# One seven-bank accumulator tile becomes four tiles, with the order list and the slot list made anew

## The chip, the cores and the metric

The kernel runs on one core of one Trainium2 chip. The metric is device microseconds of one execution, from the first to the last instruction of the program with what lies around them. The time before is 926.73 us, the median of 3 runs (922.49 to 929.71).

## The reference, cut to what matters

Attention inside hash buckets, then a mixture-of-experts step for the 128 best tokens of each batch:

```
q_bits, k_bits = (q @ proj > 0), (k @ proj > 0)          # proj: 64 x 6, so 64 buckets
mask   = bucket(q)[:, None] == bucket(k)[None, :]
scores = where(mask, q @ k.T / 8, -1e9)                  # 32 heads, 768 x 768
attn   = exp(scores - max) / (sum + 1e-9);  o = attn @ v  # 768 x 64 per head
x      = heads side by side                               # 4 batches, 768 x 512
top    = 128 best of x @ w_gate, per batch
out    = x;  out[top] += sigmoid(score) * (relu(x[top] @ w1) @ w2)   # w1 512 x 1024, w2 1024 x 512
```

## The kernel before, in words

All matmul results live in PSUM, eight banks of 512 fp32 columns. One bank is the tile `av` (output of attention). The other seven are one tile named `seven` (L198). `bank()` (L200) hands out one bank of it, `bank2()` (L203) two banks, which need not be neighbours; which ones is read digit by digit from the string BANKS.

The work is a list of short words in the string ORDER, 1955 of them, run from left to right. Each word calls a small function that issues a few instructions; each engine executes its own instructions in exactly that order, and an engine that waits holds up everything behind it. A framework adds the waits between engines from the tiles that the instructions read and write. No loop stands around the heads: words of neighbouring heads are mixed by hand or by a planner. For head h the words are:

- `xh`, `xl` (L413, L418): the fp32 input X is split in a high and a low fp16 part, on ScalarE (ACT) and VectorE (DVE). `h`, `sg`, `ss` hash four heads at once (TensorE L333, ACT L342, DVE L358). `ps`, `pa`, `pb` are DMAs on SyncE's queue (L425) that put signs, high parts and low parts into the operand buffers A (four of them) and B (three). `kv` (L518) forms on DVE the difference of the two halves of the keys.
- `mx`, `re`, `ma`, `rd`, three times each: the row maxima. `mx` (TensorE L526, two matmuls of 385 columns) takes two banks; `re` (ACT L533) is a relu in place; `ma` (TensorE L542) adds two more matmuls to the same banks, which gives the larger of the two halves; `rd` (DVE L552) takes the maximum of each row. `mt` (TensorE L560, one bank), `mc2` (ACT L565) and the DMA `mr` turn the maxima into a row of A.
- `s`, `e`, six times each: scores minus maximum. An even `s` (TensorE L586 and L589, four matmuls of 512 columns) takes two banks and is read by `e` (ACT L606, exp); an odd one (four of 256 columns) takes one bank (ACT L602). The result is P in SBUF.
- `r` (DVE L619) or `g` (GpSimd, POOL, L622): the low part R of P. `a`, six times (TensorE L644, 18 matmuls of 65 columns, with one of 396 columns, L631, ahead of the first): attention output into `av`. `rc`, `nw` (DVE) divide.
- `sv`, `sh`, `sl` for every second head: sums of v (TensorE L482, one bank).
- `w`, `c0` to `c3`, `e0` to `e3`: pieces of generators that load weights, choose the 128 tokens of a batch and run the expert on them (L872, L894: matmuls of 128 and 512 columns; one bank for each of their results). Those of the last batch come after all heads.

Of the kernel before, what the change touches and what calls it, by code (L numbers as in the profile page):

```python
# [52 lines left out]
re.1.2 ps.2.0 ma.1.1 ia.3 rd.1.1 s.0.0 ma.1.2 s.0.2 ps.2.1 xh.4 pb.2.1 rd.1.2 kv.2 e.0.0 r.0.0 s.0.3 e.0.2 X.15
ps.3.0 ps.3.1 e.0.3 s.0.4 mt.1 mc2.1 s.0.5 xl.4 mx.2.1 mx.2.2 e.0.4 re.2.1 pb.1.0 a.0.0 xl.6 mx.2.0 re.2.2 e.0.5
pb.3.3 ma.2.1 re.2.0 a.0.1 ma.2.2 mr.1 rd.2.1 s.1.1 X.7 s.1.4 e.1.1 xh.7 g.0.1 pb.3.0 rd.2.2 ma.2.0 s.1.3 s.1.0
V.1 pb.3.2 rd.2.0 e.1.4 kv.3 mt.2 e.1.0 r.0.2 mc2.2 a.0.2 s.1.2 xl.7 a.0.3 mx.3.1 xl.5 e.1.2 pa.4.0 s.1.5 pb.2.0
X.8 re.3.1 a.0.4 e.1.5 mx.3.2 mr.2 ma.3.1 r.1.0 e.1.3 h.1.0.4 rd.3.1 pa.4.1 s.2.5 re.3.2 ma.3.2 a.0.5 mx.3.0 w
rd.3.2 pb.4.3 sg.1.0.4 vh.1 s.2.4 pb.3.1 ss.1.0.4 rc.0 re.3.0 g.1.1 e.2.5 s.2.1 ps.4.1 e.2.4 pb.4.1 ps.5.1 ma.3.0
s.2.0 nw.0 rd.3.0 s.2.2 kv.4 mt.3 ps.4.0 s.2.3 pb.4.2 pa.5.1 e.2.0 pa.5.0 mx.4.0 vl.1 e.2.1 e.2.2 re.4.0 pa.6.1
X.11 mc2.3 pb.5.0 a.1.0 r.2.0 a.1.1 pa.6.0 pb.5.3 mx.4.1 e.2.3 re.4.1 mr.3 lg ps.6.0 r.1.2 a.1.2 sv.1 g.2.1 mx.4.2  # L60
sh.1 w pb.4.0 re.4.2 a.1.3 sl.1 ma.4.1 ma.4.0 a.1.4 V.2 rd.4.1 s.3.3 a.1.5 ps.5.0 ma.4.2 s.3.4 w rd.4.0 s.3.0
xh.11 e.3.3 X.10 rd.4.2 xh.8 s.3.1 rc.1 e.3.4 s.3.2 e.3.1 nw.1 e.3.0 mt.4 a.2.0 mc2.4 s.3.5 a.2.1 a.2.2 kv.5 e.3.2
# [1035 lines left out]
```

## Time and profile before

| | |
|---|---|
| median of 3 runs | 926.73 us |
| profiled execution, its own time | 927.88 us |
| its span, first to last instruction | 926.0 us |
| instructions | 13583 |
| TensorE matmul (PE) busy | 601.0 us |
| DVE busy | 357.2 us |
| ACT busy | 302.9 us |
| POOL busy | 130.4 us |
| mean granted TensorE clock | 0.679 of 2.4 GHz |

Busy time is the union of an engine's instructions; matmuls are pipelined and their ends are modelled, so a run of matmuls reads a little longer than what it adds to the path. The granted clock has two levels, 1.2 and 2.4 GHz, so a mean of 0.68 says that TensorE had the full clock for about a third of the time.

### The profile page before, as it was taken

To read this page: it belongs to the slowest core of one execution; us is meant where nothing else is said; L and a number is where in the kernel's file an instruction comes from. 1 tells how busy PE (TensorE), PEld (TensorE's weight loads), DVE (VectorE), ACT (ScalarE), POOL (GpSimd) and SP (SyncE) were. 2 spreads that over 40 slices of the span, in tenths; PEclk is the share of its full clock that TensorE was granted. 3 is DMA by queue.
4 is the path that set the end of the run, shared out by engine and by line. 5 is a ranking of instruction groups with operands and counts; after the bars stand their busy time and mean duration, and the time that the engine had idled before them with its cause. 6 is when DMAs were issued, how large, how long until landed. Compare 5 with 4: busy or idle time off the path is not lost.

```text
span 926.0 us, 13583 instructions
## 1 busy us (share of the span) xinstructions
PE 601.0 (65%) x5727; PEld 371.6 (40%) x5734; DVE 357.2 (39%) x585; ACT 302.9 (33%) x433; POOL 130.4 (14%) x91
## 2 busy tenths in 40 slices
...
DMA packets 32940, 53.32 MB, mean 58 GB/s; under 512 B 5226, under 2 KB 24176, under 8 KB 32880
## 3 DMA queue, kind: packets, MB, share of 16 engines
q1 hardware_dynamic: 21696, 32.92, 13.1%
...
q0 software_dynamic: 640, 2.10, 0.7%
q8 instruction: 45, 0.74, 0.3%
...
## 4 chain that ended last, share of the span: by engine, by line
PE 55%; ACT 24%; DVE 12%; issue 6%; DMA 2%; SPq 1%; ACTq 0%; POOLq 0%; DVEq 0%
PE seven L586 13%; PE seven L589 11%; ACT P L606 9%; PE av L644 9%; DVE m L552 9%; ACT seven L533 7%; PE seven L526 6%; PE seven L542 6%; ACT P L602 5%; PE seven L872 2%; PE seven L894 2%; PE seven L333 2%; DMA X<-in_qk_dram 1%; PE seven L482 1%; ACT sg L342 1%
## 5 line engine op out<-in xcount | busy, mean ns | idle before, releaser
L586 PE MATMUL seven<-A 97*128 97x256 f16 (+1 forms) x384 | 172.6, 455 | 130.6 <-DVE m L552 36.8
L552 DVE TENSOR_REDUCE m<-seven 128x2 fp32r<-128x770 f32 x96 | 91.3, 959 | 321.7 <-PE seven L542 84.5
L644 PEld LDWEIGHTS <-P 128*128 128x128 bf16 x2304 | 165.4, 117 | 35.9 <-issue 28.7
L589 PE MATMUL seven<-B 128*128 128x256 f16 (+1 forms) x384 | 176.4, 466 | 0.0
L644 PE MATMUL av<-V,P 128*128 128x65 f16 (+1 forms) x2304 | 169.5, 221 | 0.0
L622 POOL TENSOR_TENSOR R<-P 128x1536 f16<-128x1536 f32 x32 | 89.8, 2807 | 525.5 <-DVE R L619 114.7
L644 PE MATMUL av<-V,R 128*128 128x65 f16 x1152 | 161.4, 219 | 0.0
L606 ACT ACTIVATE P<-seven 128x1024 f32<-128x1024 f32 x96 | 97.4, 1022 | 184.5 <-PE seven L589 84.4
L644 PEld LDWEIGHTS <-R 128*128 128x128 f16 x1152 | 131.3, 117 | 0.0
L619 DVE TENSOR_TENSOR R<-P 128x1536 f16<-128x1536 f32 x64 | 111.9, 1751 | 49.7 <-ACT P L606 25.0
L589 PEld LDWEIGHTS <-B 128*128 128x128 f16 x384 | 46.9, 122 | 184.7 <-issue 174.7
L533 ACT ACTIVATE seven<-seven 128x770 f32<-128x770 f32 x96 | 76.5, 797 | 129.3 <-PE seven L589 40.7
L602 ACT ACTIVATE P<-seven 128x512 f32<-128x512 f32 x96 | 56.3, 596 | 168.9 <-PE seven L589 74.9
L542 PE MATMUL seven<-A 96*128 96x385 f16 x192 | 61.6, 416 | 52.7 <-ACT seven L533 23.4
L526 PE MATMUL seven<-kd,A 96*128 96x385 f16 x192 | 64.6, 439 | 36.4 <-ACT seven L533 9.3
L586 PEld LDWEIGHTS <-A 97*128 97x128 f16 x384 | 49.8, 130 | 55.4 <-issue 37.7
L542 PEld LDWEIGHTS <-A 96*128 96x128 f16 x192 | 20.3, 113 | 72.7 <-issue 62.2
L526 PEld LDWEIGHTS <-A 96*128 96x128 f16 x192 | 20.0, 117 | 52.6 <-issue 47.3
L872 PE MATMUL seven<-xth,w1h 128*128 128x128 f16 x128 | 24.3, 254 | 15.3 <-ACT P L606 4.6
L418 DVE SCALAR_TENSOR_TENSOR XL<-X,XH 128x768 f16<-128x768 f32 x32 | 31.3, 995 | 3.4 <-ACT XH L413 3.4
L413 ACT ACTIVATE XH<-X 128x768 f16<-128x768 f32 x32 | 26.5, 835 | 3.7 <-DMA X<-in_qk_dram 3.6
L872 PEld LDWEIGHTS <-w1h 128*128 128x128 f16 x256 | 23.7, 116 | 4.5 <-DVE xtl L848 2.1
...
## 6 DMA issues: line engine op xcount, KB each, us to landing
...
```

The source lines that it names most:

```text
L526: nc.tensor.matmul(pt[:, i, : HS + 1], a[0:96, 0, q0 : q0 + P], kd, start=True, stop=False, skip_group_check=True,)
L533: nc.scalar.activation(o, o, AF.Relu)
L542: nc.tensor.matmul(pt[:, i, : HS + 1], a[0:96, 0, q0 : q0 + P], a[0:96, 1, HS : S + 1], start=False, stop=True, skip_group_check=True,)
L552: nc.vector.tensor_reduce(st["m", h][:, 2 * t : 2 * t + 2], st["mx", h, t][:, :, : HS + 1], axis=AX.X, op=ALU.max)
L586: nc.tensor.matmul(o, a[:, 1, k0 : k0 + P], a[:, 0, q0 : q0 + n], start=True, stop=False,)
L589: nc.tensor.matmul(o, bt[:, 1, k0 : k0 + P], bt[:, 0, q0 : q0 + n], start=False, stop=True,)
L602: nc.scalar.activation(pp[:, :, 512:S], pt.rearrange("p (a b) -> p a b", a=2), AF.Exp, scale=ES)
L606: nc.scalar.activation(pp[:, :, 0:512], pt, AF.Exp, scale=ES)
L619: mine(nc.vector.tensor_tensor(**rest(h, g)))
L622: turn(nc.gpsimd.tensor_tensor(**rest(h, g)))
L644: nc.tensor.matmul(o[:, t, 0:n], l, vv[:, c, hh, v0 : v0 + n], start=False, stop=last and l is lo, skip_group_check=True,)
L872: nc.tensor.matmul(hp[:, j * P : (j + 1) * P], l[:, k, f : f + P], r[:, k * P : (k + 1) * P], start=first, stop=t["u", e] == 48, skip_grou ...
```

## The change: what it does, and the diff

Three things change. The tile `seven` is replaced by four tiles in the same seven banks: `two0`, `two1`, `two2` of two banks each and `one` of one bank. `bank()` now takes the first bank of any of the four, `bank2()` both banks of one of the first three. The string BANKS has one digit for each taking of a tile (377) where it had one for each bank (580). ORDER holds the same 1955 words in another order, so every instruction of before is there, none is new, and the order on each engine and each DMA queue is another.

```diff
 ORDER = """
...
-V.14 rd.28.2 kv.29 e.27.3 pb.28.1 a.25.5 c2 s.27.2 rc.25 nw.25 c2 s.27.5 mt.28 e.27.2 e.27.5 s.27.4 s.27.0 mc2.28
...
+c2 e.27.0 pa.30.0 ps.30.1 s.27.3 c2 s.27.2 kv.29 ps.29.0 pb.29.1 e.27.3 c2 mt.28 a.25.4 s.27.4 c2 mc2.28 r.26.0
...
 BANKS = """
-0123401423 5601240163 5012453624 3560312450 6513206213 0634512340 6534125634 1201345602 1301235641 2035146213
...
+2131203102 1320310321 2032310302 1320300230 1231302301 2102310132 1302130221 2310213203 2130121303 2012312030
...
     banks = iter("".join(BANKS.split()))
-    seven = pp7.tile([P, 7, 512], F32, name="seven")
+    slots = [pp7.tile([P, 2, 512], F32, name=f"two{i}") for i in range(3)]
+    slots.append(pp7.tile([P, 1, 512], F32, name="one"))

     def bank(name=None):
-        return seven[:, int(next(banks))]
+        return slots[int(next(banks))][:, 0]

     def bank2(name=None):
-        i, j = sorted((int(next(banks)), int(next(banks))))
-        return seven[:, i : j + 1 : j - i]
+        return slots[int(next(banks))][:, 0:2]
```

A stretch of the new order, for one head's worth of work, with the tile that each word takes in brackets (0 to 2 are `two0` to `two2`, 3 is `one`; DMA words left out): mx.10.1[0] re.10.1 rd.9.0 rc.6 g.7.1 s.8.5[3] s.8.0[1] ma.10.1 rd.9.2 e.8.5 e.8.0 mx.10.0[2] mt.9[3] mc2.9 nw.6 a.7.0 s.8.3[3] a.7.1 e.8.3 rd.10.1 mx.10.2[0] a.7.2 xl.12 s.8.2[1] a.7.3 re.10.0 r.8.2 a.7.4 a.7.5 re.10.2 e.8.2 r.8.0 ma.10.0 ma.10.2 kv.11 rc.7.

## Rows read from the trace of the kernel before

**Rows 1.** The page's head: span; an engine's busy time, share, instructions
```profile
span 926.0 us, 13583 instructions
...
PE 601.0 (65%) x5727; PEld 371.6 (40%) x5734; DVE 357.2 (39%) x585; ACT 302.9 (33%) x433; POOL 130.4 (14%) x91
```

**Rows 2.** The chain that ended last: shares by engine, then by line
```profile
PE 55%; ACT 24%; DVE 12%; issue 6%; DMA 2%; SPq 1%; ACTq 0%; POOLq 0%; DVEq 0%
PE seven L586 13%; PE seven L589 11%; ACT P L606 9%; PE av L644 9%; DVE m L552 9%; ACT seven L533 7%; PE seven L526 6%; PE seven L542 6%; ACT P L602 5%; PE seven L872 2%; PE seven L894 2%; PE seven L333 2%; DMA X<-in_qk_dram 1%; PE seven L482 1%; ACT sg L342 1%
```

**Rows 3.** Groups of instructions by line: busy us, mean ns | idle before, releaser
```profile
L552 DVE TENSOR_REDUCE m<-seven 128x2 fp32r<-128x770 f32 x96 | 91.3, 959 | 321.7 <-PE seven L542 84.5
...
L533 ACT ACTIVATE seven<-seven 128x770 f32<-128x770 f32 x96 | 76.5, 797 | 129.3 <-PE seven L589 40.7
```

**Rows 4.** Who waited for whom: us in total, times, longest us
```profile
DVE m L552 <- PE seven L542: 84.5, 25, 10.2
DVE m L552 <- PE seven L589: 62.4, 18, 8.8
DVE m L552 <- ACT P L602: 39.4, 12, 9.2
ACT P L602 <- DVE m L552: 31.2, 10, 4.8
ACT P L606 <- PE seven L526: 24.8, 13, 3.8
PE seven L542 <- ACT seven L533: 23.4, 20, 3.4
```

**Rows 5.** Timeline from 433 to 442: start, us, engine, line [idle before <-releaser]
```profile
433.26 1.02 ACT L606 ACTIVATE P<-seven 128x1024 f32<-128x1024 f32 x1 [1.79 <-PE seven L872]
434.33 0.49 PE L526 MATMUL seven<-kd,A 96*128 96x385 f16 x2 [0.56 <-ACT P L606]
434.85 1.02 ACT L606 ACTIVATE P<-seven 128x1024 f32<-128x1024 f32 x1 [0.57 <-PE seven L526]
435.93 0.22 PE L872 MATMUL seven<-xth,w1h 128*128 128x128 f16 x1 [1.11 <-ACT P L606]
...
437.83 1.63 ACT L533 ACTIVATE seven<-seven 128x770 f32<-128x770 f32 x2
...
441.15 0.51 SPq L425 DMA_DIRECT2D A<-XH  x1
```

**Rows 6.** Stretches: PE, PEld, DVE, ACT, POOL busy (instructions); PEclk, DMA share, GB/s
```profile
0.00:44.00 44.00, 18.12 (x98) 9.03 (x99) 17.58 (x31) 17.48 (x22) 11.20 (x35) 0.74 0.44 125
44.00:886.00 842.00, 562.88 (x5442) 345.72 (x5448) 327.41 (x518) 282.72 (x405) 117.25 (x54) 0.67 0.19 54
872.00:886.00 14.00, 12.92 (x239) 9.94 (x239) 6.64 (x24) 2.54 (x3) 3.75 (x2) 0.91 0.01 2
886.00:926.00 40.00, 20.01 (x187) 16.87 (x187) 12.17 (x37) 2.74 (x6) 1.96 (x2) 0.74 0.17 60
```

**Rows 7.** Pieces of the chain in order of time: start, us, what
```profile
29.52 2.12 PE seven L333 x12
...
409.77 1.34 PE seven L872 x24
...
413.57 0.34 PE seven L526 x2
...
861.12 0.54 PE av L644 x18
...
862.10 0.22 PE seven L586
...
872.17 0.33 PE av L631
...
901.33 20.25 issue
```

**Rows 8.** The tile seven, one line's instructions: ns minimum/median/maximum
```profile
L606 ACT ACTIVATE P<-seven x96: 996/1023/1035, 49.7 to 877.0; 128x1024 f32<-128x1024 f32 x96
```

More of the change, by code (lines that the diff above doesn't have):

```diff
@@ L53 @@
[L53 to L62, printed above, removed]
@@ new lines @@
+xh.7 e.1.2 ps.3.1 kv.3 e.1.3 X.8 s.1.0 mt.2 xl.7 mc2.2 a.0.2 s.1.5 vh.1 a.0.3 mx.3.1 h.1.0.4 e.1.0 re.3.1 r.0.2
+mr.2 mx.3.2 X.11 ma.3.1 e.1.5 a.0.4 sg.1.0.4 s.2.3 X.10 w vl.1 rd.3.1 pa.4.0 ss.1.0.4 mx.3.0 r.1.0 re.3.2 e.2.3
+s.1.4 a.0.5 e.1.4 ps.5.1 pb.3.1 rc.0 ps.4.0 pb.4.3 s.2.1 ma.3.2 re.3.0 ps.4.1 xh.9 s.2.4 e.2.4 w ma.3.0 nw.0
+rd.3.2 a.1.0 e.2.1 a.1.1 s.2.5 rd.3.0 g.1.1 kv.4 s.2.0 pb.3.0 r.1.2 e.2.5 mt.3 mx.4.2 V.2 s.2.2 mc2.3 a.1.2 a.1.3
+r.2.2 w mr.3 pa.6.1 e.2.0 mx.4.1 re.4.2 e.2.2 re.4.1 ma.4.2 ps.5.0 a.1.4 s.3.5 pa.5.0 pa.5.1 ma.4.1 r.2.0 w e.3.5
@@ new lines @@
+rd.4.2 w pb.5.0 mx.4.0 kv.5 X.22 a.1.5 sv.1 g.2.1 pb.4.2 s.3.2 rd.4.1 re.4.0 vh.2 sh.1 e.3.2 rc.1 pb.4.1 s.3.0
+sl.1 nw.1 ma.4.0 s.3.3 s.3.1 e.3.0 a.2.0 e.3.1 rd.4.0 mt.4 ps.6.1 w s.3.4 pa.7.0 e.3.3 a.2.1 pb.5.3 mc2.4 mx.5.1
+r.3.0 xl.9 e.3.4 mx.5.2 a.2.2 re.5.1 pb.4.0 mx.5.0 mr.4 ma.5.1 re.5.2 pa.7.1 pb.5.2 a.2.3 ps.7.0 re.5.0 pa.6.0
+vl.2 kv.6 ma.5.2 a.2.4 rd.5.1 ma.5.0 pb.6.2 rd.5.2 xh.11 sv.2 s.4.3 s.4.4 lg w a.2.5 g.3.1 e.4.3 sh.2 rd.5.0 X.15
+mt.5 sl.2 ps.6.0 rc.2 s.4.5 e.4.4 mc2.5 e.4.5 s.4.0 xh.8 s.4.2 w xl.11 s.4.1 pb.5.1 mx.6.2 e.4.0 mr.5 pb.6.3 e.4.2
@@ new lines @@
+nw.2 a.3.0 re.6.2 r.3.2 mx.6.0 r.4.2 ps.7.1 mx.6.1 xl.8 a.3.1 e.4.1 re.6.0 re.6.1 ma.6.2 w a.3.2 xh.10 rd.6.2
+s.5.5 pb.6.0 ma.6.0 a.3.3 V.3 kv.7 g.4.1 a.3.4 rd.6.0 mx.7.0 ma.6.1 re.7.0 rd.6.1 s.5.1 e.5.1 a.3.5 ma.7.0 w rc.3
+pb.7.3 nw.3 e.5.5 mt.6 s.5.4 mc2.6 s.5.0 e.5.4 s.5.3 rd.7.0 pb.6.1 mr.6 vh.3 pb.7.2 r.4.0 e.5.0 s.6.2 s.5.2 w
+xl.10 pb.8.3 e.6.2 po.0.0 a.4.0 h.2.0.4 e.5.3 a.4.1 sg.2.0.4 mx.7.1 a.4.2 w s.6.5 a.4.3 pa.8.0 r.5.0 pa.9.1 X.14
+pa.9.0 r.5.2 ss.2.0.4 ps.9.0 a.4.4 s.6.4 re.7.1 e.5.2 e.6.5 vl.3 ps.8.1 pb.7.1 mx.7.2 ma.7.1 pa.8.1 rd.7.1 a.4.5 w
@@ new lines @@
+e.6.4 ps.8.0 pb.8.2 rc.4 s.6.3 g.5.1 s.6.1 nw.4 re.7.2 e.6.3 ma.7.2 pb.7.0 s.6.0 e.6.1 pb.8.0 sv.3 rd.7.2 xh.15
+kv.8 X.16 sh.3 a.5.0 e.6.0 a.5.1 mx.8.2 mt.7 pb.9.2 mx.8.1 a.5.2 sl.3 V.4 mc2.7 mx.8.0 pb.9.0 r.6.2 re.8.2 mr.7
+a.5.3 ma.8.2 ps.9.1 w pa.10.1 re.8.0 re.8.1 r.6.0 ps.10.1 xh.14 pa.10.0 a.5.4 ma.8.0 rd.8.2 pb.9.3 s.7.3 w ps.10.0
+kv.9 ma.8.1 e.7.3 s.7.0 a.5.5 rd.8.1 w rd.8.0 s.7.5 s.7.1 e.7.0 vh.4 g.6.1 mx.9.1 e.7.5 rc.5 re.9.1 nw.5 s.7.2
+e.7.1 a.6.0 ma.9.1 a.6.1 e.7.2 s.7.4 mt.8 a.6.2 mx.9.0 pb.8.1 w a.6.3 vl.4 pb.10.2 xl.14 r.7.0 mc2.8 a.6.4 mr.8 w
@@ new lines @@
+e.7.4 pa.11.0 ps.11.1 mx.9.2 rd.9.1 w re.9.0 s.8.4 re.9.2 ma.9.0 s.8.1 X.12 r.7.2 e.8.4 pb.9.1 xl.15 w ps.11.0
+a.6.5 ma.9.2 pb.10.3 e.8.1 kv.10 xh.12 mx.10.1 X.17 re.10.1 rd.9.0 rc.6 pa.11.1 g.7.1 pb.10.1 s.8.5 s.8.0 ma.10.1
+rd.9.2 e.8.5 e.8.0 mx.10.0 mt.9 mc2.9 pb.10.0 nw.6 X.13 a.7.0 mr.9 s.8.3 a.7.1 e.8.3 rd.10.1 mx.10.2 a.7.2 V.5
+xl.12 s.8.2 a.7.3 re.10.0 r.8.2 a.7.4 a.7.5 re.10.2 e.8.2 r.8.0 pb.11.3 ma.10.0 ma.10.2 kv.11 rc.7 xh.13 sv.4 w
+s.9.4 sh.4 pb.11.2 vh.5 rd.10.0 s.9.0 pb.11.1 sl.4 pa.12.1 s.9.3 e.9.4 pb.11.0 mx.11.1 e.9.0 e.9.3 nw.7 a.8.0
@@ new lines @@
+re.11.1 g.8.1 rd.10.2 mt.10 c0 s.9.2 a.8.1 mc2.10 s.9.5 w e.9.5 xl.13 c0 ma.11.1 h.3.0.4 e.9.2 rd.11.1 s.9.1 vl.5
+mx.11.0 pa.12.0 c0 mr.10 e.9.1 a.8.2 pa.13.1 c0 re.11.0 mx.11.2 c0 a.8.3 ma.11.0 a.8.4 s.10.5 c0 re.11.2 r.9.0
+ma.11.2 w a.8.5 c0 sg.3.0.4 ss.3.0.4 rd.11.0 rc.8 s.10.0 xh.16 w ps.12.1 s.10.4 g.9.1 e.10.5 s.10.3 nw.8 rd.11.2
+a.9.0 e.10.0 a.9.1 e.10.4 sv.5 s.10.1 mt.11 mc2.11 c0 c0 a.9.2 ps.12.0 s.10.2 mr.11 kv.12 pb.13.3 ps.13.1 sh.5
+r.9.2 a.9.3 e.10.3 pa.14.1 e.10.1 sl.5 pb.12.0 e.10.2 mx.12.2 r.10.0 s.11.2 ps.13.0 c0 re.12.2 e.11.2 a.9.4 s.11.5
@@ new lines @@
+c0 w e.11.5 pb.12.2 ma.12.2 pb.12.3 mx.12.0 rd.12.2 c0 re.12.0 mx.12.1 c0 a.9.5 ma.12.0 pb.13.2 ps.14.1 g.10.1
+re.12.1 pa.13.0 s.11.4 ma.12.1 rd.12.0 e.11.4 V.6 rc.9 nw.9 c0 pb.13.1 c0 rd.12.1 pb.12.1 pa.14.0 s.11.0 s.11.1
+a.10.0 a.10.1 kv.13 e.11.1 mt.12 mx.13.1 c0 e.11.0 a.10.2 s.11.3 mc2.12 mx.13.0 pb.13.0 re.13.1 r.10.2 mr.12
+e.11.3 ma.13.1 pb.14.1 ps.14.0 rd.13.1 a.10.3 mx.13.2 ps.15.1 s.12.3 re.13.0 pa.15.0 re.13.2 ma.13.0 s.12.2 e.12.3
+r.11.0 e.12.2 a.10.4 ma.13.2 xh.17 a.10.5 rd.13.0 c0 s.12.5 rd.13.2 w g.11.1 c0 s.12.1 s.12.0 rc.10 nw.10 r.11.2
@@ new lines @@
+e.12.1 vh.6 e.12.0 a.11.0 e.12.5 s.12.4 a.11.1 X.18 kv.14 mx.14.1 e.12.4 a.11.2 mt.13 r.12.0 pb.15.0 e0 mx.14.2
+vl.6 re.14.1 mc2.13 ma.14.1 a.11.3 pa.16.0 a.11.4 pb.15.2 sv.6 e0 pa.16.1 mx.14.0 w rd.14.1 mr.13 re.14.2 pb.14.2
+ma.14.2 ps.15.0 g.12.1 sh.6 w rd.14.2 s.13.1 re.14.0 a.11.5 pa.15.1 X.19 ma.14.0 w s.13.0 rc.11 sl.6 w pb.14.0
+kv.15 rd.14.0 e.13.1 nw.11 xh.18 s.13.4 s.13.3 e.13.0 s.13.5 e.13.3 mx.15.0 xh.19 pb.15.3 a.12.0 r.12.2 e.13.5
+mt.14 xl.19 xl.17 a.12.1 e.13.4 a.12.2 mc2.14 mx.15.2 pb.14.3 X.27 xl.16 re.15.0 a.12.3 s.13.2 re.15.2 a.12.4 V.7
@@ new lines @@
+pa.17.1 w a.13.5 rd.16.0 e.15.2 vh.8 mx.16.2 ps.17.1 kv.17 re.16.2 rc.13 e0 pb.16.0 nw.13 s.15.1 e0 pa.18.1 s.15.0
+e.15.1 ma.16.2 w g.15.1 pb.16.1 s.15.4 r.14.0 e.15.0 pa.18.0 ps.19.1 rd.16.2 a.14.0 ps.18.1 a.14.1 e0 w mt.16 vl.8
+e0 mx.17.2 a.14.2 mc2.16 a.14.3 e.15.4 e0 pb.17.0 mx.17.0 xh.22 re.17.2 r.15.2 mr.16 re.17.0 ma.17.2 V.9 a.14.4
+s.16.3 pa.19.0 w pb.18.2 pb.18.3 X.21 a.14.5 rd.17.2 e.16.3 e0 mx.17.1 re.17.1 ma.17.0 r.15.0 s.16.0 ma.17.1
+pb.17.3 pb.17.1 kv.18 e0 rc.14 rd.17.0 s.16.1 ps.19.0 nw.14 e.16.0 mx.18.2 rd.17.1 e0 pa.19.1 e.16.1 a.15.0 e0
@@ new lines @@
+xh.21 X.24 s.16.2 mt.17 mx.18.1 re.18.2 ma.18.2 mc2.17 re.18.1 xh.20 a.15.1 r.16.0 pb.18.0 s.16.5 rd.18.2 a.15.2
+mx.18.0 ma.18.1 e.16.2 a.15.3 xl.21 re.18.0 mr.17 a.15.4 kv.19 xl.22 ma.18.0 e.16.5 mx.19.1 sv.8 rd.18.1 po.1.0
+rd.18.0 sh.8 a.15.5 s.16.4 sl.8 vh.9 rc.15 e.16.4 nw.15 s.17.3 re.19.1 s.17.0 a.16.0 e.17.3 X.25 a.16.1 s.17.2
+g.16.1 pb.19.3 vl.9 ma.19.1 r.16.2 c1 rd.19.1 a.16.2 e.17.0 pb.19.2 c1 mx.19.2 X.28 mt.18 a.16.3 e.17.2 g.17.1
+re.19.2 c1 xl.20 s.17.4 s.17.1 mc2.18 pb.19.1 pb.19.0 pb.18.1 e.17.4 a.16.4 ma.19.2 mr.18 mx.19.0 rd.19.2 e.17.1
@@ new lines @@
+a.18.0 rd.20.2 e.19.4 pb.21.0 a.18.1 mx.21.1 mt.20 r.18.2 e.19.1 e.19.3 c1 mc2.20 re.21.1 pb.20.3 ps.22.1 mx.21.2
+c1 a.18.2 mx.21.0 c1 re.21.2 mr.20 ps.22.0 ma.21.1 c1 re.21.0 pb.21.3 ma.21.2 vh.10 kv.22 a.18.3 c1 ma.21.0
+rd.21.1 c1 c1 pb.21.2 a.18.4 xh.24 rd.21.2 rd.21.0 s.19.5 g.19.1 s.19.0 e.19.5 s.20.3 pa.23.1 a.18.5 s.20.5 e.19.0
+mt.21 mc2.21 mr.21 rc.18 s.20.2 e.20.5 pa.23.0 s.20.0 s.20.4 e.20.3 s.20.1 e.20.2 nw.18 r.19.0 pa.24.0 e.20.4
+a.19.0 mx.22.2 e.20.0 mx.22.0 pb.22.2 re.22.0 ps.23.1 a.19.1 vl.10 re.22.2 ps.23.0 s.21.0 ma.22.0 e.20.1 a.19.2
@@ new lines @@
+r.19.2 e.21.0 a.19.3 r.20.2 ma.22.2 c1 xh.27 sv.10 rd.22.0 mx.22.1 pb.23.3 pb.22.0 sh.10 re.22.1 xh.26 c1 r.20.0
+a.19.4 s.21.3 g.20.1 sl.10 e.21.3 rd.22.2 a.19.5 ma.22.1 s.21.2 rc.19 nw.19 s.21.4 e.21.2 s.21.5 pb.23.2 pb.22.3
+rd.22.1 kv.23 e.21.4 xl.26 a.20.0 s.21.1 pa.25.1 xl.27 mt.22 mc2.22 mx.23.1 xl.24 xl.25 pa.24.1 a.20.1 a.20.2
+e.21.5 mx.23.0 re.23.1 ma.23.1 e.21.1 e1 X.30 a.20.3 pb.23.1 pb.22.1 mr.22 rd.23.1 pa.25.0 re.23.0 e1 h.6.0.4 X.31
+ma.23.0 a.20.4 mx.23.2 rd.23.0 sg.6.0.4 e1 s.22.1 s.22.0 a.20.5 re.23.2 pb.24.1 r.21.0 e1 e1 ma.23.2 ss.6.0.4
@@ new lines @@
+e.22.1 g.21.1 V.11 s.22.3 rc.20 e1 e.22.0 s.22.5 vh.11 rd.23.2 e1 ps.24.1 pb.24.0 mt.23 mc2.23 pb.23.0 nw.20
+e.22.3 vl.11 e.22.5 a.21.0 kv.24 xh.30 e1 s.22.4 w ps.24.0 sv.11 a.21.1 X.29 mr.23 r.21.2 e.22.4 s.23.0 sh.11 e1
+mx.24.0 a.21.2 e.23.0 a.21.3 mx.24.1 sl.11 ps.25.1 re.24.0 re.24.1 a.21.4 ma.24.0 r.22.2 a.21.5 s.23.5 mx.24.2
+re.24.2 ma.24.1 rd.24.0 rd.24.1 s.22.2 ma.24.2 e.23.5 kv.25 e1 e1 xh.29 e1 V.12 e.22.2 rd.24.2 mt.24 ps.26.1
+pb.24.3 s.23.3 r.22.0 ps.25.0 pb.24.2 rc.21 mc2.24 pa.26.1 nw.21 e.23.3 e1 s.23.4 s.23.2 vh.12 e.23.4 e.23.2
@@ new lines @@
+pb.25.1 a.22.0 g.22.1 ps.26.0 a.22.1 mr.24 mx.25.0 r.23.2 g.23.1 re.25.0 mx.25.1 pb.25.2 a.22.2 vl.12 re.25.1
+a.22.3 a.22.4 s.23.1 ma.25.1 ma.25.0 e1 s.24.5 pb.25.0 e.23.1 rd.25.1 e1 pa.26.0 r.23.0 s.24.3 e.24.5 mx.25.2
+e.24.3 pb.25.3 xl.29 V.13 e1 s.24.4 e1 re.25.2 ma.25.2 a.22.5 kv.26 pb.26.3 e1 rd.25.0 e.24.4 rd.25.2 xh.31 s.24.2
+pa.27.0 r.24.2 e.24.2 s.24.0 e1 rc.22 e.24.0 pa.27.1 sv.12 sh.12 nw.22 s.24.1 a.23.0 xl.30 mx.26.1 e1 e.24.1 e1
+sl.12 mt.25 re.26.1 mx.26.2 e1 r.24.0 xh.28 ps.27.1 pb.27.3 mc2.25 re.26.2 ma.26.1 mx.26.0 ma.26.2 a.23.1 re.26.0
@@ new lines @@
+a.23.2 mr.25 ma.26.0 e1 rd.26.1 kv.27 rd.26.2 a.23.3 pb.27.2 a.23.4 a.23.5 vh.13 pb.26.0 ps.27.0 s.25.4 rd.26.0
+s.25.2 rc.23 e.25.4 g.24.1 pb.26.2 mt.26 nw.23 s.25.1 c2 mc2.26 e.25.2 e.25.1 a.24.0 pb.26.1 mx.27.0 a.24.1 s.25.5
+xl.28 s.25.0 mr.26 re.27.0 xl.31 c2 po.2.0 ma.27.0 c2 h.7.0.4 e.25.0 sg.7.0.4 pa.28.0 rd.27.0 a.24.2 vl.13 c2
+ss.7.0.4 a.24.3 mx.27.2 a.24.4 mx.27.1 ps.28.1 e.25.5 r.25.0 re.27.2 s.25.3 c2 pb.27.1 ma.27.2 rd.27.2 pa.28.1
+e.25.3 c2 a.24.5 s.26.2 re.27.1 sv.13 ma.27.1 e.26.2 s.26.0 sh.13 e.26.0 s.26.4 rc.24 pb.28.3 pa.29.1 rd.27.1
@@ new lines @@
+rd.29.2 s.28.5 e.28.5 a.26.0 mx.29.0 a.26.1 pb.29.2 re.29.0 s.27.5 a.26.2 ma.29.0 a.26.3 r.26.2 mx.29.1 r.27.0
+re.29.1 pb.30.2 a.26.4 vh.14 e.27.5 s.28.0 a.26.5 rd.29.0 vl.14 rc.26 ma.29.1 pa.31.0 nw.26 pb.30.0 ps.31.1
+pa.31.1 s.28.2 s.28.3 e.28.0 s.28.1 e.28.2 pb.29.0 rd.29.1 kv.30 r.27.2 a.27.0 e.28.3 e.28.1 a.27.1 mx.30.2 a.27.2
+mx.30.0 mt.29 V.15 r.28.0 re.30.2 mx.30.1 mc2.29 re.30.1 ma.30.2 rd.30.2 sv.14 a.27.3 a.27.4 mr.29 ma.30.1 g.28.1
+rd.30.1 a.27.5 re.30.0 rc.27 nw.27 s.29.1 ma.30.0 sh.14 ps.31.0 e.29.1 s.29.0 e.29.0 kv.31 sl.14 vh.15 sc.3.0.0.1
```

134 lines of the change are left out of this document (32 added, 102 removed), and 8 rows, old and new, of the table BANKS.

## The prediction, made before the changed kernel was run

> **What bounds the kernel now.** I read the page's head first: in a span of 926.0 us no engine is busy for more than 65% (TensorE 601.0), DVE for 39% and ACT for 33% [rows 1]. So no engine's sum is the bound, and the question is why they don't run beside each other. The chain of waits comes next. It is shared out as TensorE 55%, ACT 24%, DVE 12% [rows 2], and by line it holds nearly everything that ACT and DVE do on `seven`: the row maximum L552 has 9% of 926, that is 83 us, of the 91.3 us that all of them take; the relu L533 has 7%, 65 of 76.5 us [rows 2, 3]. Where engines overlap, only some of an engine's operations are on the path. Here almost all are: the engines take turns.
>
> The list of waits says at what. A row maximum needs the matmuls L542, but it also stood 62.4 us for L589, a score matmul, and 39.4 us for L602, an exp; an exp (L602) stood 31.2 us for a row maximum, another (L606) 24.8 us for L526, a matmul of the maxima [rows 4]. None of these pairs passes data. The timeline shows one turn after the other: the exp of 433.26 ends at 434.28, L526 starts at 434.33; it ends at 434.82, the next exp starts at 434.85; that ends at 435.87, and the expert's matmul L872, which continues a sum in a bank it already holds, starts at 435.93 after 1.11 us of idling [rows 5]. Could two of these share a bank? No: what L526 wrote at 434.33 is not read until the relu at 437.83, and had it gone where the exp of 434.85 reads, the scores would have been overwritten first [rows 5]. So an access of one engine to `seven` waits for the last access of another engine to any bank of it. The kernel is bound by one token, the tile, which goes from engine to engine in the order of the list.
>
> One rule speaks against the change. The Trainium skill, "PSUM — Partial Sum Buffer", PSUM bank collisions raise a hardware error, says that accesses of two engines to different banks run clean and that guarding by bank is enough. Were the waits of before guarded so, seven separate banks would already be free of each other, and four tiles could only be fewer buffers; that is the third rival below. The rows above disagree with it as a description of this kernel's waits: what is safe by bank is ordered here by tile.
>
> **The change part by part.** *Instructions:* the same words, so nothing is added to any engine: zero. *Operand shapes:* pairs of banks become neighbours. The exp over a pair took 996 to 1035 ns over all the distances that BANKS gives [rows 8], so that is worth 2% of an exp at most, either way: zero. *DMA order:* about ten DMAs per head are moved on SyncE's queue, one issue taking 0.51 us [rows 5], 5 us a head against the 16 us a head expected below; the DMA engines go from a share of 0.19 [rows 6] to 0.19 x 926/600 = 0.29. Both stay covered; a cover of 11 us a head on SyncE would have to go before they cost. POOL's 117 us [rows 6] are covered likewise.
>
> *The waits between banks* go, and that is the whole change. I work out the middle, 44 to 886, 842 us [rows 6], and keep the start (44 us, loads and the first hash) and the end (40 us: choice and expert of the last batch, 20.25 us of it after the gather [rows 7]) as they are, since there each step needs the one before.
>
> First, TensorE's own work in the middle at full clock, from pieces of the chain at that clock [rows 7]. Per head 12 matmuls of 512 columns at 0.22 and 12 of 256 at half of that, 3.96; six pairs of 385 columns at 0.34, 2.04; six `a` at 0.54, 3.24; L631 0.33. Sum 9.57, times 32 is 306 us. Three experts: 96 L872 (1.34 per 24) and 24 L894 (512 columns, 0.22), 10.6 each, 32 us. Hashes: 186 matmuls at 2.12 per 12, halved because that piece ran at the low clock, 16 us. Sums of v and turned maxima I put at 9 us (estimate, 48 short groups of about the 0.2 us of a 512-column matmul). Together 363 us. Check: at the clock of before, 0.67 of full, 363/0.67 = 542, against 563 us busy, which counts the pipelines' ends [rows 6].
>
> Second, the clock. Before, TensorE is busy for two thirds of the middle at 0.67. Where it is busy for 12.92 of 14 us, the clock granted is 0.91 [rows 6]. After the change I expect it busy for some 85%, so 0.85, nearer the second row: 363/0.85 = 427 us. The ends are 0.67 (542 us) and 0.95 (382 us).
>
> Third, the idle time of TensorE that stays. True needs stay: the second maxima matmuls waiting for their relu, 23 us before [rows 4]. New is the wait for a tile: of 344 times that a word of the heads' stages takes a tile again, the new order has 65 with no TensorE word between the reader that frees it and the word that takes it, and 83 with one. The first kind waits for about one read of 0.96 us (the row maximum [rows 3]): 62 us; the second, for half of that if uncovered, 40 us. Behind such a wait stands everything later on TensorE, and ACT's exps with it. I take 23 + 62 = 85 us; ends 23 and 125.
>
> Sum: 44 + 40 + 427 + 85 = 596 us of span, and 2 us around it (own time 927.88 against 926.0): 598, say 600, 16 us per head. The profiled execution is 1.2 us above the median of 926.73, which I neglect. What is late next: DVE, with 327 us in the middle, and ACT with 283 [rows 6], 64% and 55% of 512.
>
> **Rivals.** *The clock does not rise.* Fewer tiles mean many short gaps on TensorE, and it stays at the 0.67 that it had with gaps everywhere: 84 + 542 + 85 + 2 = 713 us. For it: long stretches of before sit low. Against it: the dense stretch at 0.91 [rows 6]. The Trainium skill, "TensorE: Matmul & The Clock Gate", A second HAM failure mode: psum-queue depth-cycling, tells of a kernel whose cycling through PSUM banks kept the clock going up and down, which would give this same 713; no row here shows four tiles.
>
> *Nearly full overlap.* `a` words stand between most words that take a tile, so TensorE waits only for its relus: 84 + 382 + 23 + 2 = 491 us. Against it: DVE would then be busy for 327 of 405 us, in order, with row maxima behind low parts of P.
>
> *Slots too few: slower.* The three double tiles are taken 281 times, 8.8 a head, 2.9 each. A taking lasts at least one maxima chain, 2 x (0.34 + 0.05) + 0.80 + 0.05 + 0.96, some 2.6 us at full clock and 3.3 at half. If relu and row maximum stand so long in ACT's and DVE's queues that a tile is held for 9.3 us, a head takes 27 us and the run 84 + 32 x 27 + 2 = 950 us. The point is a mean hold of 9.0 us (842/32 = 26.3 us a head, over 2.9). For it: with four tiles never more than four results are open, where seven banks held up to seven. Against it: three times the bare hold is needed, and what delays ACT and DVE most today is the token itself [rows 4].
>
> *The change does not do what it says.* If the four tiles were still ordered as one, the turns would stay: the new order has 670 changes of engine among accesses to PSUM where the old has 648 (counted in the lists, over the heads' words and the experts and choices of the first three batches), each worth some 0.05 us of handing over plus a pipeline's end, 22 x 0.2 = 4 us, so 927 to 935 us. For it: whatever ties bank to bank might tie tile to tile. Against it: `av` is a tile of its own in the same memory, and `a` runs while `seven` is handed about.
>
> **How the numbers follow.** Forecast (530 to 680, 600): 0.52. Clock stays low (680 to 760): 0.20. Nearly full overlap (under 530): 0.19. Too few slots: 0.05. Still one: 0.04. The likeliest is 600. From 500 to 740 the range holds the forecast whole, most of the low-clock case and about half of the full overlap, some 0.8, and reaches nearly to the ends of the unknowns, 491 and 84 + 542 + 125 + 2 = 753. About 1%, 917 to 936, is what this kernel's measurement can tell from no change. Faster: 0.52 + 0.20 + 0.19 = 0.91; within 1% the last case, 0.04; slower 0.05.
>
> **What would show it.** Right: no row maximum waits for an exp or for L589 any more, and no exp for L526; the chain keeps well under 83 us of L552; the granted clock is above 0.8; what TensorE still waits for is a reader of the tile it takes, or its relu. DVE's and ACT's busy times stay at 357 and 303 us. Wrong: waits across tiles persist; or the clock stays near 0.67 with TensorE busy for over 80% (first rival); or the maxima's tiles are held for 9 us, with TensorE idle ahead of L526 and L586 for row maxima (third). A time of 480 or less would mean that the work itself was counted too high.

## The result, and the profile after

The changed kernel takes 431.95 us (median of 4 runs, 427.59 to 435.39) against 925.2 us of the kernel before on the same chip: a ratio of 0.465 with a 95% interval of 0.461 to 0.470. A second session, beside the experiments, gave 428.65 us against 926.2, 0.464 (0.461 to 0.466). The forecast was 600 with a range of 500 to 740: the direction was right, and the time lies 68 us below the range.

The rows that follow are from the profiled execution of the second session (own time 431.01 us, span 429.2); the first session's profile is of its slow run, 435.39 us, which the ratio leaves out. The page's head, the granted clock in 40 slices, and the chain's shares:

```profile
span 429.2 us, 13616 instructions
...
PE 389.2 (91%) x5726; PEld 278.6 (65%) x5734; DVE 351.2 (82%) x585; ACT 289.0 (67%) x433; POOL 136.5 (32%) x91
...
PEclk9999999999899998999999999899999999999569
...
PE 62%; DVE 10%; DMA 10%; issue 8%; SPq 4%; ACT 4%; POOL 1%; POOLq 0%; DVEq 0%; ACTq 0%
PE av L642 19%; PE two L584 9%; PE two L587 9%; PE two L540 5%; PE two L524 5%; SPq L423 3%; PE two L870 3%; DMA X<-in_qk_dram 3%; DVE m L550 2%; PE one L892 2%; DMA xe<-out_dram,idx 2%; PE one L584 2%; DVE R L617 2%; PE one L587 2%; DVE cm L736 2%
```

Lines have moved up by two: L550 is the row maximum (L552 before), L531 the relu (L533), L524 and L540 the matmuls of the maxima (L526, L542), L584 and L587 those of the scores, L604 and L600 the exps. The work is the same as in [rows 1]: DVE 351 us against 357, ACT 289 against 303. TensorE is down from 601 to 389 us, most of it by the clock, which went from 0.679 to 0.964: 601 x 0.679/0.964 is 423. On the chain ACT has gone from 24% of 926 to 4% of 429, that is from 222 to 17 us, and the row maxima from 83 us [rows 2] to 2%, some 10 us. DMA and its queue SPq have gone the other way, from 3% of 926 to 14% of 429, that is from 28 to 60 us. The engines no longer take turns; TensorE is most of the path.

The stretches up to the first score matmul, from there to the last attention output, and behind it (columns as in [rows 6]):

```profile
0.00:24.00 24.00, 14.07 (x93) 6.99 (x93) 17.54 (x30) 14.39 (x19) 10.60 (x35) 0.93 0.72 192
24.00:395.50 371.50, 356.45 (x5447) 255.50 (x5454) 321.21 (x516) 271.86 (x409) 123.50 (x54) 0.99 0.44 125
395.50:429.20 33.70, 18.64 (x187) 16.13 (x187) 12.49 (x39) 2.74 (x6) 2.40 (x3) 0.75 0.21 71
```

In the middle TensorE is busy for 356.45 of 371.5 us, at 0.99 of its clock. The waits of DVE, ACT and TensorE, to hold beside [rows 4]: us in total, times, longest.

```profile
DVE m L550 <- PE two L540: 14.0, 15, 2.2
...
ACT P L604 <- PE two L587: 24.7, 37, 4.7
ACT two L531 <- PE two L524: 13.9, 19, 1.9
...
PE two L540 <- ACT two L531: 2.8, 3, 2.1
PE two L524 <- ACT P L604: 2.2, 2, 1.4
...
PE two L524 <- DVE m L550: 0.8, 1, 0.8
PE two L584 <- DVE m L550: 0.8, 3, 0.3
```

Each of the large ones is now an engine waiting for the data that it works on: the maximum for its matmuls, the exp for its scores, the relu for its matmuls. The maximum that stood 62.4 us for score matmuls and 39.4 us for an exp [rows 4] waits for no score matmul, and once, 0.7 us, for an exp. And TensorE's waits for a tile to come free, the last three rows, are 3.8 us in all. The timeline shows the same at work (start, us, engine, line):

```profile
206.89 0.93 DVE L550 TENSOR_REDUCE m<-two 128x2 fp32r<-128x770 f32 x1
207.03 0.49 PE L540 MATMUL two<-A 96*128 96x385 f16 x2
...
207.23 1.02 ACT L604 ACTIVATE P<-two 128x1024 f32<-128x1024 f32 x1 [0.34 <-PE two L587]
207.36 0.38 PE L892 MATMUL one<-w2h,hth 128*128 128x512 f16 x1
```

Between 206.9 and 208.2 a row maximum, an exp, matmuls of the maxima and the expert's matmuls run side by side in four tiles; in [rows 5] the same kinds stood one behind the other.

### The profile page after: what moved, and what is told of

Its sections match the earlier page's. It is cut to its first block, busy times and chain, and to the rows that moved or that the text cites. A ratio compares the mean times of both kernels' runs of the same rounds, so it can differ in the third digit from the quotient of the medians.

```text
span 433.6 us, 13616 instructions
## 1 busy us (share of the span) xinstructions
PE 391.2 (90%) x5726; PEld 279.6 (64%) x5734; DVE 349.9 (81%) x585; ACT 288.8 (67%) x433; POOL 135.5 (31%) x91
## 4 chain that ended last, share of the span: by engine, by line
PE 61%; DMA 13%; DVE 9%; issue 7%; SPq 5%; ACT 4%; POOL 1%; POOLq 0%; DVEq 0%; ACTq 0%
PE av L642 19%; PE two L584 9%; PE two L587 9%; PE two L540 5%; PE two L524 5%; SPq L423 4%; DMA B<-XL 3%; PE two L870 2%; DMA X<-in_qk_dram 2%; PE one L892 2%; PE one L584 2%; DMA A<-mr 2%; PE one L587 2%; DVE m L550 2%; DVE R L617 2%
## 5 line engine op out<-in xcount | busy, mean ns | idle before, releaser
L642 PEld LDWEIGHTS <-P 128*128 128x128 bf16 x2304 | 121.1, 98 | 19.6 <-issue 1.7
L642 PE MATMUL av<-V,P 128*128 128x65 f16 (+1 forms) x2304 | 127.2, 194 | 0.0
L642 PE MATMUL av<-V,R 128*128 128x65 f16 x1152 | 121.9, 193 | 0.0
L604 ACT ACTIVATE P<-two 128x1024 f32<-128x1024 f32 x96 | 97.0, 1019 | 29.3 <-PE two L587 28.2
L617 DVE TENSOR_TENSOR R<-P 128x1536 f16<-128x1536 f32 x64 | 113.0, 1779 | 3.1 <-ACT P L604 2.4
L550 DVE TENSOR_REDUCE m<-two 128x2 fp32r<-128x770 f32 x96 | 90.5, 953 | 20.0 <-PE two L540 16.7
L584 PE MATMUL two<-A 97*128 97x512 f16 (+1 forms) x272 | 93.6, 352 | 1.7 <-DMA A<-mr 0.9
L587 PE MATMUL two<-B 128*128 128x512 f16 (+1 forms) x272 | 93.4, 351 | 0.0
L531 ACT ACTIVATE two<-two 128x770 f32<-128x770 f32 x96 | 74.9, 795 | 19.5 <-PE two L524 18.1
L584 PEld LDWEIGHTS <-A 97*128 97x128 f16 x384 | 38.1, 99 | 30.9 <-DMA A<-mr 7.5
L587 PEld LDWEIGHTS <-B 128*128 128x128 f16 x384 | 38.0, 99 | 24.6 <-issue 3.1
L524 PE MATMUL two<-kd,A 96*128 96x385 f16 x192 | 46.8, 335 | 5.0 <-DMA A<-sg 1.8
L540 PE MATMUL two<-A 96*128 96x385 f16 x192 | 47.4, 331 | 2.6 <-ACT two L531 2.5
L600 ACT ACTIVATE P<-one 128x512 f32<-128x512 f32 x56 | 33.1, 591 | 11.5 <-PE one L587 11.4
L584 PE MATMUL one<-A 97*128 97x256 f16 x112 | 28.7, 279 | 4.3 <-DMA A<-XH 2.3
L600 ACT ACTIVATE P<-two 128x512 f32<-128x512 f32 x40 | 23.7, 592 | 9.7 <-PE two L587 9.4
L587 PE MATMUL one<-B 128*128 128x256 f16 x112 | 28.6, 279 | 1.6 <-DMA B<-XL 1.6
L540 PEld LDWEIGHTS <-A 96*128 96x128 f16 x192 | 16.1, 98 | 11.7 <-issue 3.9
```

Of the source, the lines that this page charges most:

```text
L524: nc.tensor.matmul(pt[:, i, : HS + 1], a[0:96, 0, q0 : q0 + P], kd, start=True, stop=False, skip_group_check=True,)
L531: nc.scalar.activation(o, o, AF.Relu)
L540: nc.tensor.matmul(pt[:, i, : HS + 1], a[0:96, 0, q0 : q0 + P], a[0:96, 1, HS : S + 1], start=False, stop=True, skip_group_check=True,)
L550: nc.vector.tensor_reduce(st["m", h][:, 2 * t : 2 * t + 2], st["mx", h, t][:, :, : HS + 1], axis=AX.X, op=ALU.max)
L584: nc.tensor.matmul(o, a[:, 1, k0 : k0 + P], a[:, 0, q0 : q0 + n], start=True, stop=False,)
L587: nc.tensor.matmul(o, bt[:, 1, k0 : k0 + P], bt[:, 0, q0 : q0 + n], start=False, stop=True,)
```

## The experiments

Where no number of runs is given, a kernel below ran once. To judge single runs by: the changed kernel's ten runs of both sessions lie between 426.93 and 435.39 us, and all runs of the kernel before between 915.82 and 933.93.

**The new order with one tile.** The theory: the tile is a token. Rival: the new order is what made it fast.

```diff
-    slots = [pp7.tile([P, 2, 512], F32, name=f"two{i}") for i in range(3)]
-    slots.append(pp7.tile([P, 1, 512], F32, name="one"))
+    seven = pp7.tile([P, 7, 512], F32, name="seven")
+    slots = [seven[:, 2 * i : 2 * i + 2] for i in range(3)] + [seven[:, 6:7]]
```

> New order and new slot list, the same seven banks and the same neighbouring pairs, but as slices of one tile. Theory (the tile is a token: an access of one engine waits for the last access of another engine to any bank of the same tile): the turns come back, 670 changes of engine against the 648 of before, so 900 to 970 us, a granted clock near 0.68, row maxima again waiting for exps and score matmuls. Rival (the new order is what made it fast): within 5% of the changed kernel, under 455 us.

Measured: 936.04 us, beside 927.01 for the kernel before. Same banks, same neighbouring pairs, same order as the changed kernel; only that the four slots are slices of one tile. Its head and its waits:

```profile
span 934.3 us, 13583 instructions
...
PE 599.1 (64%) x5734; PEld 370.8 (40%) x5734; DVE 355.2 (38%) x585; ACT 304.1 (33%) x433; POOL 131.5 (14%) x91
```

```profile
DVE m L550 <- PE seven L587: 102.9, 20, 10.5
DVE m L550 <- PE seven L540: 84.5, 25, 7.7
...
ACT seven L531 <- PE seven L587: 40.0, 15, 5.9
...
ACT P L600 <- DVE m L550: 32.8, 11, 5.5
```

The waits without data are all back: the maximum for score matmuls (102.9 us), the exp for a maximum, the relu for score matmuls. The new order by itself is worth nothing with one tile; that it costs 1% is not shown by one run, 2 us above the slowest of the kernel before. It is also what the case "the change does not do what it says" would have cost: four tiles ordered as one.

**The old order with four tiles.** The tiles and `bank()` are those of the change. Slots go to the first free tile, single banks to `one` where it is free; of the 1955 words of the old list 28, which found no tile free, are moved back by 1 to 8 places. One such place (`s.2.3` and `mx.4.0`, three places each):

```diff
...
-s.2.2 kv.4 mt.3 ps.4.0 s.2.3 pb.4.2 pa.5.1 e.2.0 pa.5.0 mx.4.0 vl.1 e.2.1 e.2.2 re.4.0
+s.2.2 kv.4 mt.3 ps.4.0 pb.4.2 pa.5.1 e.2.0 s.2.3 pa.5.0 vl.1 e.2.1 e.2.2 mx.4.0 re.4.0
...
```

> The order list of before with the four tiles; slots are given out first free, and 28 words that found no free tile are moved back by 1 to 8 places. Theory (token): most of the gain is there without the new order, 440 to 520 us, TensorE busy for 75 to 90%, clock over 0.9. Rival (the new order is what made it fast): over 800 us. Rival (four tiles are too few for an order made for seven banks): 550 to 750 us, with TensorE waiting for readers of the tile it takes.

Measured: 462.66 us, TensorE busy for 85%, clock 0.978.

```profile
PE two L580 <- ACT P L600: 6.3, 14, 0.8
PE two L580 <- DVE m L546: 5.5, 8, 1.6
```

All three numbers are as the theory had them. So the tiles bring 927 to 463 us with nearly the old order, and the new order with its slot list the rest, 463 to about 430 (7%). An order made for seven banks waits some 12 us for exps and maxima before it takes a tile for scores (the rows above); that rival shows, but small.

**Two tiles, and three.** The same list and slots, the slots grouped into fewer tiles.

```diff
...
+    four = pp7.tile([P, 4, 512], F32, name="four")
+    three = pp7.tile([P, 3, 512], F32, name="three")
+    slots = [four[:, 0:2], four[:, 2:4], three[:, 0:2], three[:, 2:3]]
```

> New order and slot list, the same banks, in two tiles of four and three banks, two slots each. Theory (token): two tokens, so an access waits for a foreign access about half as often; between the two ends, 550 to 750 us, clock 0.75 to 0.9. Rival (order alone): under 455 us. Rival (bank distance or shape of the slots): no change from four tiles.

```diff
...
+    slots = [pp7.tile([P, 2, 512], F32, name=f"two{i}") for i in range(2)]
+    three = pp7.tile([P, 3, 512], F32, name="three")
+    slots += [three[:, 0:2], three[:, 2:3]]
```

> New order and slot list, the same banks, in three tiles: two of two banks, and one of three banks that holds the third pair and the single bank. Theory (token): only the last pair and the single wait for each other; 450 to 560 us, less than with two tiles, more than with four. Rival (order alone): under 455 us.

Measured: 568.64 and 479.87 us, clock 0.928 and 0.975. With one and four tiles this is a scale: 936, 569, 480, 429 us. Both times lie where the theory had them; two tiles have the clock a little higher than I expected (0.75 to 0.9). In the kernel with two tiles TensorE waits again, in the tile `four` above all: for the relus of its own chains (L532, 12.2 us where four tiles have 2.8), and for readers before it takes a tile for scores (L585).

```profile
PE four L541 <- ACT four L532: 12.2, 17, 1.3
PE four L585 <- DVE m L551: 11.0, 11, 2.7
...
PE four L585 <- ACT P L605: 7.3, 6, 1.8
```

With three tiles the waits for readers have moved to `three`, the one that still holds two slots:

```profile
PE three L585 <- DVE m L551: 5.8, 9, 1.4
...
PE three L585 <- ACT P L601: 3.6, 7, 0.7
```

**The price of the clock in the kernel before.** Idle matmuls fill TensorE's gaps, into columns of `av` that nothing reads: a new word `fl`, five matmuls of 116 columns, stands behind 152 words of TensorE whose next access to `seven` is another engine's (one line of the list is shown).

```diff
+FILL = 5
...
+    def fill():
+        for i in range(FILL):
+            nc.tensor.matmul(
+                st["Ob", st["h"]][:, NC * OW :], ones16, ones16[:, : 512 - NC * OW],
+                start=False, stop=False, skip_group_check=True,
+            )
...
-re.22.2 ma.22.2 a.19.3 r.20.0 re.22.1 xl.24 e1 ps.23.1 e.20.2 a.19.4 pb.23.3 a.19.5 rd.22.2 sv.10 e1 ma.22.1
+re.22.2 ma.22.2 fl a.19.3 r.20.0 re.22.1 xl.24 e1 fl ps.23.1 e.20.2 a.19.4 pb.23.3 a.19.5 rd.22.2 sv.10 e1 ma.22.1
```

> The kernel of before, one tile and old order, with five idle matmuls of 116 columns into unused columns of av at 152 places where TensorE hands the tile over to another engine: more work for TensorE, in its gaps, at no turn. If the low clock is a part of the cost of the turns, the granted clock rises from 0.68 to 0.75 or more and the time falls to 850 to 900 us, though work is added. If the clock has no part in it, 926 to 960 us.

Measured: 880.67 us, 46 less than the kernel before, with 760 matmuls more. The stretch from 44 to 845 in this kernel (columns as in [rows 6]):

```profile
44.00:845.00 801.00, 545.57 (x6219) 361.47 (x6225) 331.04 (x530) 284.91 (x409) 117.23 (x54) 0.80 0.21 58
```

The clock rose from 0.67 to 0.80, though TensorE is busy for about the same share, 68% here and 67% in [rows 6]. So the turns cost twice: the engines wait, and TensorE, which idles in between, does its own part at a lower clock. But the second is the smaller: TensorE's 55% of the chain [rows 2], 509 us, would at 0.99 in place of 0.67 take 509 x 0.67/0.99 = 344 us, 165 less (an estimate), of the 497 us that the change brought.

**What is bound now.** One product of three is left out of the attention output (high part of P by low part of v).

```diff
-            for l, n, v0 in ((hi, D + 1, 0), (hi, D, D + 2), (lo, D + 1, 0)):
+            for l, n, v0 in ((hi, D + 1, 0), (lo, D + 1, 0)):
```

> The changed kernel without the middle one of the three products of the attention output (high part of P by low part of v), 1152 of 3456 matmuls with their weight loads, so the output lacks that small term. They take 0.54 us per 18 at full clock, 35 us in all. If TensorE is the bound now, 392 to 402 us; if DVE (busy for 81%) or the waits for tiles are, 415 us or more.

Measured: 422.25 us, 6 less than the changed kernel's 428.65 and 5 less than its fastest run, where TensorE as the only bound promised 27 to 37. TensorE's busy time fell by 22 us (389.2 to 366.7), and its place on the chain went to DVE:

```profile
by line: DVE R L617 11.0%; issue 10.7%; DVE m L550 8.1%; PE av L642 5.6%; PE two L584 5.0%; PE two L587 4.4%; PE two L540 3.5%; PE two L524 3.2%; DVE XL L416 2.8%; SPq L423 2.8%; DMA xe<-out_dram,idx 2.3%; DMA X<-in_qk_dram 2.3%; ACT two L5
```

The low part of P (L617), at the head of this line, had 2% of the chain in the changed kernel. So TensorE is not the only bound: it is on the path of the changed kernel for most of the time, and DVE stands right behind it.

**Whether the readers of a tile have slack.** Every relu of the maxima runs twice.

```diff
         nc.scalar.activation(o, o, AF.Relu)
+        nc.scalar.activation(o, o, AF.Relu)
```

> The changed kernel with every relu of the maxima run twice in place (96 more of 0.80 us, 77 us more for ACT, which then is busy for some 365 us): the same values, and each double tile of a maxima chain held 0.8 us longer. If the readers of the tiles have slack because TensorE sets the pace, the time grows by less than 15 us, to 430 to 445. If a tile taken again waits for its reader, as the prediction had it, most of the 77 us shows: 480 to 505 us.

Measured: 463.95 us, 35 more, which neither theory had. The waits tell the two apart all the same:

```profile
PE two L541 <- ACT two L532: 30.7, 54, 1.3
...
PE two L524 <- ACT P L605: 2.2, 3, 1.3
...
PE two L585 <- ACT P L605: 0.7, 2, 0.4
```

L532 is the second relu and L541 the second matmuls of the same chain. TensorE waits 30.7 us for its own relu, a need of the data, where the list leaves too little between `mx` and `ma`. For taking a tile again (L524, L585) it waits no more than before, though each tile of the maxima is held 0.8 us longer. So the takings have slack; the chain inside a tile has less.

**A faster tail.** Eight matmuls of 512 columns are queued while TensorE waits for the last gather (the word `wl`, and its bank in the second list).

```diff
-sc.3.1.3.4 rc.31 c3 nw.31 c3 c3 c3 c3 c3 c3 c3 c3 c3 c3 c3 c3 c3 c3 c3 c3 c3 c3 c3 c3 c3 c3 c3 po.3.0 c3 c3 c3 e3
+sc.3.1.3.4 rc.31 c3 nw.31 c3 c3 c3 c3 c3 c3 c3 c3 c3 c3 c3 c3 c3 c3 c3 c3 c3 c3 c3 c3 c3 c3 c3 po.3.0 c3 c3 c3 wl e3
...
-2121032312 3013023102 1021320323 1023010323 1212301130 3022102202 1032302230 2323230
+2121032312 3013023102 1021320323 1023010323 1212301130 3022102202 1032302230 23123230
```

> The changed kernel itself, beside the one with the warmed tail on the same chip: 428 to 435 us by both theories.

> The changed kernel with eight matmuls of 512 columns on two1, put on TensorE's queue behind the last choice, where it stands idle for 3.85 us for the gather. If the last expert is slow because TensorE comes to it at the low clock (0.50 from 404 to 418, 0.70 to 422), its 48 first matmuls go from about 5.2 us to 2.7: 2 to 3 us less than the changed kernel. If the clock rises at the same time whatever stands ahead, or the expert waits for its operands, no change.

Measured: 425.68 us (6 runs) against 428.65 (6 runs), ratios to the kernel before of 0.462 (0.459 to 0.464) and 0.464 (0.461 to 0.466). The piece of the chain behind the gather, in the changed kernel and then in this one:

```profile
409.41 15.42 issue
```

```profile
405.65 12.80 issue
```

And the same stretches with TensorE's clock (columns as in [rows 6]):

```profile
409.41:424.83 15.42, 14.29 (x148) 13.06 (x148) 4.30 (x10) 1.78 (x4) 0.00 (x0) 0.79 0.00 1
```

```profile
405.65:418.46 12.81, 11.57 (x148) 10.48 (x148) 4.30 (x10) 1.78 (x4) 0.00 (x0) 1.00 0.01 1
```

The last expert is 2.6 us shorter in these two profiles, with the same 148 matmuls at 1.00 of the clock in place of 0.79, as expected; for the whole time the intervals overlap, so that 3 us are gained is likely and not shown.

**More work for POOL.** In every fourth head `r.h.2` becomes `g.h.2` (a third of that head's low part of P goes from DVE to POOL), on top of the warmed tail. Two of the eight places:

```diff
-nw.2 a.3.0 re.6.2 r.3.2 mx.6.0 r.4.2 ps.7.1 mx.6.1 xl.8 a.3.1 e.4.1 re.6.0 re.6.1 ma.6.2 w a.3.2 xh.10 rd.6.2
+nw.2 a.3.0 re.6.2 g.3.2 mx.6.0 r.4.2 ps.7.1 mx.6.1 xl.8 a.3.1 e.4.1 re.6.0 re.6.1 ma.6.2 w a.3.2 xh.10 rd.6.2
...
-e.7.4 pa.11.0 ps.11.1 mx.9.2 rd.9.1 w re.9.0 s.8.4 re.9.2 ma.9.0 s.8.1 X.12 r.7.2 e.8.4 pb.9.1 xl.15 w ps.11.0
+e.7.4 pa.11.0 ps.11.1 mx.9.2 rd.9.1 w re.9.0 s.8.4 re.9.2 ma.9.0 s.8.1 X.12 g.7.2 e.8.4 pb.9.1 xl.15 w ps.11.0
```

> The kernel with the warmed tail, and in every fourth head one more low part of P computed on POOL in place of DVE (8 of 64: DVE 14 us less, POOL 23 us more). If DVE paces the stretches in which TensorE waits, 418 to 424 us. If TensorE alone sets the pace, or the slower POOL delays the attention output, 425 us or more.

Measured: 428.74 us (4 runs), ratio 0.464 (0.459 to 0.468), which is the second of the two: no gain beside the warmed tail's 0.462, and no loss that the intervals show. Whether DVE's relief or POOL's slowness decides there stays open.

## Why the prediction was wrong

The mechanism was right and the time was not. The steps that failed: the clock was read off a busy share, a wait was charged for each taking of a tile that looks tight in the list, and the start and the end were kept as they were.

**What held.** The token: shown by the kernel with the new order and one tile, 936 us with all the waits without data, and by the scale over one to four tiles. Nothing for the shapes and POOL: DVE's, ACT's and POOL's busy times stayed. TensorE's work, 363 us at full clock: it is busy for 356 in the middle at 0.99. So the sign that a time of 480 or less would mean work counted too high misleads: the time is below 480, and the work was counted about right. The zero for the DMA order is not borne out: the DMA share in the middle rose to 0.44, not 0.29, and of the 60 us that DMA and SPq have on the chain some 27 lie in the first 40 us. In the middle TensorE itself stands 4.0 us for a row of A (`PE one L584 <- DMA A<-mr`).

**What failed: three terms of the sum, all in one direction.** The forecast's 596 us of span against 429.2:

| term | forecast | measured | difference |
|---|---|---|---|
| start | 44 | 24 | -20 |
| end | 40 | 33.7 | -6 |
| TensorE in the middle | 427 (clock 0.85) | 356.5 (0.99) | -70.5 |
| its idle time there | 85 | 15 | -70 |

*The clock.* I took TensorE to be busy for 85% and read 0.85 for it from two rows, the nearer of which was 0.91 at 92% busy [rows 6]. It was busy for 96%, and had 0.99. But the share was not the main fault; reading the clock off it was. The stretches from the first score matmul to the last attention output with two tiles, with three, and with four in the old order (columns as in [rows 6]):

```profile
28.90:528.50 499.60, 397.93 (x5457) 268.45 (x5455) 322.97 (x516) 278.79 (x409) 121.53 (x54) 0.94 0.33 91
```

```profile
22.30:440.00 417.70, 368.74 (x5457) 254.81 (x5455) 323.04 (x517) 275.72 (x410) 121.35 (x54) 0.99 0.40 111
```

```profile
26.30:425.50 399.20, 362.62 (x5458) 254.11 (x5456) 326.18 (x517) 272.31 (x410) 117.89 (x54) 1.00 0.41 115
```

With two tiles TensorE is busy for 80% at 0.94, with three for 88% at 0.99, with the old order for 91% at 1.00; the kernel with idle matmuls had 0.80 at 68%. At the 85% that I forecast, the old order's whole run had 0.978: 363/0.978 is 371 us (an estimate), so some 56 of the 70.5 us come from the reading alone. The row of 0.91 was 14 us of a kernel that had 0.67 in its middle, and gave no clock for another kernel.

*The idle time.* This is the step that failed in its reasoning. I counted takings of a tile that have no TensorE word, or one, between the reader that frees the tile and the word that takes it, and let each wait for a read: 62 us, up to 102. They cost 3.8 us, and the relus, put at 23 us, cost 2.8. A place in the list is not a time: TensorE is the late engine, and when it comes to the word, the reader that stands just ahead in the list has mostly run. With the list's words laid beside the trace's instructions, 47 takings with no TensorE word behind the reader can be timed in the changed kernel (expert and choice words counted as TensorE's): the reader had ended 0.45 us before TensorE began, at the median, and in 39 of them at least 0.2 us before. The experiment with two relus agrees: longer holds, no longer waits for a tile. That the other engines' queues are emptier is my reason for it, and not measured.

*The start and the end.* I kept them because "each step needs the one before". In the start that was wrong: there too the maxima of the first heads were handed about (relus and row maxima have 4.9 and 4.8 us of the chain's first 45), and it lasts 24 us now to the first score matmul (37.7 before, and 44 where I cut the stretch). It was wrong in the end too. Of the 6 us, 1.9 were lost in the choice of the last batch and 4.8 behind the gather, from 20.25 to 15.42 us, at about the same clock. The stretch behind the gather before, and TensorE's waits in it:

```profile
901.33:921.58 20.25, 14.40 (x148) 12.81 (x148) 4.30 (x10) 1.78 (x4) 0.00 (x0) 0.82 0.00 1
```

```profile
PE seven L872 <- DVE xtl L848: 1.7, 1, 1.7
PE seven L872 <- DVE htl L884: 1.5, 1, 1.5
...
```

TensorE is busy for 14.4 us there as it is after (14.29), but idle for 5.9 where it now is for 1.1. Both waits are turns: the first matmuls of L872 need `xth`, not `xtl`, and its second half goes to a bank of its own; each time it stood until DVE had read another bank of `seven`.

**The rivals.** "Nearly full overlap", 491 us, was the right one, at a chance of 0.19, and its own terms were still too high: start and end by 26.3 us, TensorE in the middle by 25.5, its idle time by 8. "The clock does not rise" was wrong: 0.99 with only four tiles to cycle through. The clock that goes up and down by cycling through PSUM, of which the Trainium skill tells ("TensorE: Matmul & The Clock Gate", A second HAM failure mode: psum-queue depth-cycling), does not occur here; the granted clock in the slices of the changed kernel is 0.8 or more until the last three. "Slots too few" was wrong: 3.8 us of waits for a tile, and 463 us even with an order made for seven banks. "Still one" was wrong, and the kernel with one tile shows what it would have cost. The Trainium skill ("PSUM — Partial Sum Buffer", PSUM bank collisions raise a hardware error) says that accesses of two engines to different banks run clean; what runs now side by side in four tiles, from 206.89 us for one, agrees with it. Its rule of guarding by bank did not describe the waits of before, which were by tile, and no run here guards by bank alone.
